# Sliding-window attention with sinks, then an erf-softplus FFN: the first two groups' keys and queries loaded two tokens to a partition

## The chip, the cores and the metric

One core of a Trainium2 chip runs the whole program. The metric is the device time of one execution in microseconds (us); smaller is better. A core has five engines that run side by side and wait for one another by semaphores: PE (TensorE, matmuls; PEld is its weight load), DVE (VectorE), ACT (ScalarE), POOL (GpSimd) and SP (SyncE, which here only issues transfers). Each engine takes its instructions in the order in which the program lists them.

## The reference

Batch 4, 8 heads, 768 tokens, 64 elements per head; 4 sink tokens and a window of 128. All arrays are fp32 in the reference; the two weights reach the kernel as 8-byte numbers.

```python
scores = q @ k^T / sqrt(64)
keep   = (key position < n_sink) | (0 <= query - key < window)
a      = softmax over the kept keys
x      = (a @ v), heads side by side: 3072 tokens x 512
h      = x @ w_in                      # 512 -> 2048
g      = h * erf(softplus(h))
out    = g @ w_out                     # 2048 -> 512
```

## The kernel before

The tokens are worked in 12 groups of 256 (`GT`); a batch element has three groups. A group's attention runs in four steps, one for each pair of heads, so step s belongs to group s // 4; there are 48. A step consists of `prep` (transposes of keys and queries on PE, copied by ACT into `kq`), `core` or `score` (scores on PE; on DVE a predicated copy, then one instruction per block that adds the mask and takes the minimum; the exponential on ACT), `norm` (division by the sum), `ptrans` (weights transposed on PE, copied by ACT into `pa` and `pz`, triangles cut by POOL), `av` (product with the values) and `xfin` (copy into `xf`, later `xh` and `xl`). In group 0 and the other groups that begin a batch element the first 16 keys are also copied behind each block of keys (`SW`), since every query sees the sinks.

Beside it the FFN of a group runs in 16 slices of the hidden width: `hidden` (PE), `act` (ACT for tanh and squares, DVE for the polynomial) and `project` (PE). For the first two groups it works in plain fp32 with one copy of each weight (`wf`); for the others with two rounded parts (`wt`). The 32 weight blocks are loaded as 512 KB of 8-byte numbers (`wload`) and put together to fp32 by three integer instructions each on DVE (`wconv`, L543 to L551).

The order of each engine's work comes from a planner that simulates a timeline; the program gives it priorities (`at(a, what)`, with stage a and offset `O`), and `follow(prev, ins)` fixes that an instruction comes behind another on its engine. `mark["t", s]` is the last score instruction of step s on DVE, `mark["s", s]` the last one of its `norm`.

Groups 0 and 1 have early loads of their own. `early_tile` makes one tile for k, q or v of all 8 heads of a group with 128 tokens to a partition block: partition p holds tokens p and 128 + p, in the order (n h d). `early_load` issues two transfers for each, one per block of 128 tokens, in runs of 64 fp32 (256 bytes). The list `head` sets the order in which SP issues them: k and q of heads 0 and 1 (q's first on ACT's queue), of heads 2 and 3, the first weight, k and q of heads 4 to 7, v, eight transfers for the sinks' rows of v (`early_sinks`), four weights, group 1's k and q, and so on. ACT's queue also loads the two scalars n_sink and window, from which DVE makes the masks `mask0`, `mask1` and `mask`; the third mask and the flags are made by `set_rest`.

Of the kernel before, what the change touches and what calls it, by code (L numbers as in the profile page):

```python
# [14 lines left out]
ALU = mybir.AluOpType  # L15
# [4 lines left out]
P = 128  # L20
SW = 16
# [18 lines left out]
NE, AL = 4, 2  # L40
# [12 lines left out]
def kernel(  # L53
# [11 lines left out]
    nc = tc.nc  # L65
    B, H, S, D = q.shape
    NT, DM = out.shape
    DF = w_in.shape[1]
    NPAIR = H // 2
    NC = DM // P  # L70
    NF = DF // P
    GT = 256
    GPB = S // GT
    NG = B * GPB
    NU = 4
    NSTEP = NG * NPAIR
# [54 lines left out]
    def fast_path():  # L131
        with ExitStack() as st:
# [27 lines left out]
            def set_mask(mk):  # L160

                x = nc.vector.tensor_copy(mk[:, P:], kw[:, 256 : 256 + SW])
                if mk is mask:
                    follow(mark["t", 0], x)
                nc.vector.tensor_scalar(mk, mk, -1.0, NEG, op0=ALU.add, op1=ALU.mult)

            def set_rest():

                follow(mark["t", 0], nc.vector.tensor_tensor(mask[:, :P], kw[:, :128], kw[:, 128:256], op=ALU.max))
                set_mask(mask)  # L170
                set_flags(lambda ins: follow(mark["t", 0], ins))

            set_mask(mask0)
            set_mask(mask1)
# [48 lines left out]
            def early_tile(g, nm):  # L223

                t = wpool.tile([P, 2 * DM], F32, tag="wo", name=f"{nm}_early{g}")
                t = early[g, nm] = t.rearrange("p (n h d) -> p n h d", n=2, h=H)
                for c in range(NPAIR):
                    d, cs = stp.setdefault(g * NPAIR + c, {}), slice(2 * c, 2 * c + 2)
                    if nm == "v":
                        d[nm] = [early[0, nm][:, 1, cs] if g else None] + [t[:, n, cs] for n in range(2)]  # L230
                    else:
                        d[nm] = t[:, :, cs]
                return t

            def early_load(g, nm, hs, eng=None):

                t = early[g, nm] if (g, nm) in early else early_tile(g, nm)
                src = dict(q=q, k=k, v=v)[nm]
                for n in range(2):
                    r0 = g * GT + n * P  # L240
                    (nc.sync if n else eng or nc.sync).dma_start(t[:, n, hs], src[0, hs, r0 : r0 + P].rearrange("h p d -> p h d"))

            def early_sinks(z, i, h):

# [42 lines left out]
            def prep(s):  # L287

                g, c = divmod(s, NPAIR)
                d = stp[s]  # L290
                tp = ps_t.tile([P, 4, P], F32, tag="t", name=f"tqk_{s}")
                for j, t in enumerate((d["k"], d["q"])):
                    for i in range(2):
                        nc.tensor.transpose(  # L294
                            out=tp[:, 2 * j + i, :], in_=t[:, i].rearrange("p h d -> p (h d)"), identity=ident
                        )
                nc.scalar.copy(kq[:, c, 1:, :P], tp)  # L297
                if g % GPB == 0:
                    x = tp[:, 0, :SW].rearrange("p (o t) -> p o t", o=1)
                    nc.scalar.copy(kq[:, c, :3, P:], x.broadcast_to([P, 3, SW]))  # L300

            def core(s):

                prev = None
                late = s - AL >= 2 * NPAIR
                if late:
                    prev = av(s - AL)
                if s < NSTEP:
                    score(s, prev)

            def score(s, prev):

# [58 lines left out]
            def norm(s):  # L371
                d = stp[s]
                sm = d["sum"]
                follow(mark["t", 2] if s == 1 else None, nc.vector.tensor_scalar_add(sm, sm, 1.0e-9))
                nc.vector.reciprocal(sm, sm)
                for i in range(2):
                    for h in range(2):
                        p = pst[:, s % RING, i, h, :P]
                        if NM <= s < NA:
                            nc.scalar.mul(p, p, sm[:, i, h : h + 1])  # L380
                        else:
                            nc.vector.tensor_scalar_mul(p, p, sm[:, i, h : h + 1])
                snk = d["snk"] = small.tile([P, 2 * 4 * SW], F32, tag="snk", bufs=2, name=f"snk_{s}")
                x = pst[:, s % RING, :, :, P:].rearrange("p i h t -> p (i h) t").rearrange("p (o n) t -> p o n t", o=1)
                r = sm.rearrange("p i h -> p (i h)").rearrange("p (o n t) -> p o n t", o=1, t=1)
                mark["s", s] = nc.vector.tensor_tensor(
                    snk.rearrange("p (o n t) -> p o n t", o=2, t=SW), x.broadcast_to([P, 2, 4, SW]),
                    r.broadcast_to([P, 2, 4, SW]), op=ALU.mult,
                )
# [89 lines left out]
            def pos(s):  # L479

                return s if s < NE else 3 * s - 6 if s < 2 * NPAIR else 4 * s - 11

            plan = {}
            for s in range(NSTEP + AL):
                if s < NSTEP:
                    for what, fn, a in (
                        ("prep", prep, max(4, s - 1) if NE <= s < 2 * NPAIR else pos(s) - 3), ("norm", norm, pos(s) + 1 + (s == 1)), ("ptrans", ptrans, pos(s) + 2),
                        ("load", load, pos(s) - 4),
                    ):
                        if what == "load":  # L490
                            if s < 2 * NPAIR:
                                continue
                            plan.setdefault(a, []).append(("load", load_v, s))
                        plan.setdefault(max(a, 0 if what == "prep" else -1), []).append((what, fn, s))
                    if s >= 2 * NPAIR:
                        plan.setdefault(pos(s) - 2, []).append(("dup", dup, s))
                    if s // NPAIR % GPB < GPB - 1:
                        plan.setdefault(pos(s) + (2 if s < NE else 1), []).append(("kcopy", kcopy, s))
# [34 lines left out]
            def wconv(n, wn):  # L533
# [9 lines left out]
                first = nc.vector.tensor_scalar(  # L543
                    ti, w[:, :, 1], 0x07FFFFFF, 3, op0=ALU.bitwise_and, op1=ALU.logical_shift_left
                )
                follow(mark["s", 2] if wn < 1 else mark["t", 3] if wn < 3 else mark["s", 3], first)
                follow(mark.get(("c", wn - 2)), first)
                nc.vector.scalar_tensor_tensor(
                    out=ti, in0=w[:, :, 1], scalar=-0x40000000, in1=ti, op0=ALU.bitwise_and, op1=ALU.bitwise_or
# [23 lines left out]
            head = [(early_load, 0, "k", two[0]), (early_load, 0, "q", two[0], nc.scalar)]  # L573
            head += [(early_load, 0, nm, two[1]) for nm in "kq"] + [(wload, order[0])]
            head += [(early_load, 0, nm, four) for nm in "kq"] + [(early_load, 0, "v", slice(0, H))]
            head += [(early_sinks, z, i, h) for z in range(2) for i in range(2) for h in range(2)]
            head += [(wload, n) for n in order[1:4]]
            head += [(wload, order[4])] + [(early_load, 1, nm, slice(0, H)) for nm in "kq"]
            head += [(wload, n) for n in order[5:8]] + [(early_load, 1, "v", slice(0, H))] + [(wload, n) for n in order[8:W0]]
            for x, (fn, *args) in enumerate(head):  # L580
# [2 lines left out]
            for z in range(2):  # L583
                plan.setdefault(0, []).append(("kcopy", lambda s: early_dup(s), z))
            plan.setdefault(2 * NE, []).append(("dup", lambda s: next_dup(), NE))
            plan.setdefault(2, []).append(("prep", lambda s: set_rest(), NSTEP))
            for m in range(-LEAD, NG * NF + LAG + 2):
                a = m + LEAD
                live = 0 <= m < NG * NF
# [255 lines left out]
```

## Time and profile before

| | |
|---|---|
| median of 3 runs | 738.38 us (738.17 to 738.97) |
| the profiled execution | 738.16 us, span 736.5 us |
| busy, share of the span | PE 97%, PEld 81%, ACT 75%, DVE 66%, POOL 29% |
| granted PE clock, mean | 0.997 |

The span is the time from the first to the last instruction that the profiler recorded; the rest of the execution's time lies around it. Busy shares are means over the whole span and hide that the engines' loads differ by stage. In a line of the timeline the first two numbers are the start and the duration in us; "x4" is the number of instructions merged, and the bracket at the end is the idle time of the engine ahead of them and what ended it. Instructions of PE overlap, so the duration of several in a row is less than the sum of single ones.

### The profile page before, as it was taken

Reading aid. Unit: us, or ns where it says so; the run is one execution under the profiler, and the core shown is the slowest. Engines: PE = TensorE matmul, PEld = TensorE weight load, DVE = VectorE, ACT = ScalarE, POOL = GpSimd, SP = SyncE. Lnnn points to the kernel's source line nnn. Section 1 sums busy time; section 2 is a strip of 40 time slices with the busy share of each in tenths; the row PEclk is TensorE's granted clock in tenths of the full one; section 3 lists DMA queues with packets and bytes.
Section 4 is the critical chain, followed back from the end, with each engine's and each line's share of the span. In section 5 each row is a group of like instructions: output and inputs, shape, how many; then the busy total and the mean of one; then the engine's idle time right before and its main releaser. Section 6 shows DMA issues by size and latency. Waiting matters only on the chain. (4 is left out here: it accounts for less than half of the span.)

```text
span 736.5 us, 16405 instructions
## 1 busy us (share of the span) xinstructions
PE 716.0 (97%) x5808; PEld 595.6 (81%) x5808; DVE 485.3 (66%) x1367; ACT 551.9 (75%) x1313; POOL 210.1 (29%) x302
## 2 busy tenths in 40 slices
PE   6889999999999999999999999999999999999997
PEld 3666567767888888888888888888898888898885
DVE  7999997665776765665666666665566566475252
ACT  4687759976986876976976975985886886777573
POOL 3411332111323322332333232233224223233221
PEclk9999999999999999999999999999999999999999
DMA  7999011121222122212212211311321221200000
GB/s 175 279 347 377 22 37 55 31 57 40 72 48 69 45 54 48 65 43 57 67 41 56 75 38 44 84 36 40 78 48 37 79 58 35 67 13 2 29 1 34
DMA packets 113001, 53.07 MB, mean 72 GB/s; under 512 B 91728, under 2 KB 105552, under 8 KB 112912
## 3 DMA queue, kind: packets, MB, share of 16 engines
q1 hardware_dynamic: 112352, 51.87, 26.3%
q8 instruction: 49, 0.80, 0.5%
q14 instruction: 40, 0.33, 0.1%
q10 hardware_dynamic: 560, 0.07, 0.1%
HBM read 38.01 MB, written 6.29 MB: 60 GB/s over the span
## 5 line engine op out<-in xcount | busy, mean ns | idle before, releaser
L645 PE MATMUL h<-xh,wt 128*128 128x256 f32 x1408 | 277.9, 285 | 0.2 <-DVE u L667 0.2
L645 PEld LDWEIGHTS h<-xh,wt 128*128 128x128 f32 x1408 | 224.0, 188 | 7.6 <-issue 1.7
L675 POOL TENSOR_TENSOR g<-u,g 128x512 fp32r<-128x512 f32 x80 | 106.2, 1327 | 339.3 <-DVE g L674 335.4
L645 PE MATMUL h<-xl,wt 128*128 128x256 f32 x704 | 198.2, 282 | 0.0
L663 ACT ACTIVATE u<-r 128x512 f32<-128x512 f32 x288 | 161.5, 622 | 12.7 <-DVE gf L667 4.7
L645 PEld LDWEIGHTS h<-xl,wt 128*128 128x128 f32 x704 | 132.2, 188 | 5.0 <-issue 1.2
L667 DVE SCALAR_TENSOR_TENSOR u<-u,u 128x512 f32<-128x512 f32 x160 | 124.5, 778 | 16.0 <-ACT u L663 1.8
L691 PE MATMUL o<-wt,g 128*128 128x512 f32 x320 | 127.4, 398 | 0.0
L690 PE MATMUL o<-wt,g 128*128 128x512 f32 x320 | 127.3, 398 | 0.0
L692 PE MATMUL o<-wt,g 128*128 128x512 f32 x320 | 123.6, 397 | 0.2 <-POOLq L813 0.2
L667 DVE SCALAR_TENSOR_TENSOR u<-u,h 128x512 f32<-128x512 f32 x80 | 54.9, 686 | 84.5 <-ACT u L663 82.3
L416 POOL TENSOR_SCALAR_AFFINE_SELECT pz<-pa 64x256 f32<-64x256 f32 (+1 forms) x96 | 54.5, 567 | 150.8 <-ACT pa L405 147.5
L367 ACT ACTIVATE pst<-pst,neg 128x144 f32<-128x144 f32 x192 | 77.4, 407 | 24.9 <-DVE neg L363 23.9
L658 ACT ACTIVATE r<-h 128x512 f32<-128x512 f32 x96 | 56.7, 591 | 17.9 <-PE h L645 14.4
L690 PEld LDWEIGHTS o<-wt,g 128*128 128x128 f32 x320 | 60.0, 187 | 11.5 <-ACT ot L696 0.4
L692 PEld LDWEIGHTS o<-wt,g 128*128 128x128 f32 x320 | 59.0, 188 | 12.5 <-POOLq L813 0.7
L691 PEld LDWEIGHTS o<-wt,g 128*128 128x128 f32 x320 | 60.0, 188 | 10.5
L674 DVE CAST g<-u 128x512 fp32r<-128x512 f32 x80 | 34.6, 432 | 46.3 <-PE o L692 43.6
L659 ACT ACTIVATE r<-r 128x512 f32<-128x512 f32 x96 | 60.7, 632 | 2.5
L660 ACT ACTIVATE r<-r 128x512 f32<-128x512 f32 x96 | 60.7, 632 | 2.5
L687 PE MATMUL o<-wf,gf 128*128 128x512 f32 x128 | 58.3, 594 | 1.2 <-DVE gf L667 1.2
L297 ACT COPY kq<-tqk 128x512 f32<-128x512 f32 x48 | 27.9, 582 | 32.6 <-PE tqk L294 30.2
(88 smaller groups left out, 939.2 us busy)
## 6 DMA issues: line engine op xcount, KB each, us to landing
ws<-in_moe_w_in_dram SPq DMA_DIRECT2D x16, 512.0 KB, 6.0
ws<-in_moe_w_out_dram SPq DMA_DIRECT2D x16, 512.0 KB, 8.3
out_dram<-ot SPq DMA_DIRECT2D x24, 256.0 KB, 2.1
v<-in_v_dram SPq DMA_DIRECT2D x56, 96.0 KB, 2.2
q<-in_q_dram SPq DMA_DIRECT2D x80, 64.0 KB, 2.1
k<-in_k_dram SPq DMA_DIRECT2D x80, 64.0 KB, 2.1
vz<-v SPq DMA_DIRECT2D x80, 64.0 KB, 2.1
kq<-kq SPq DMA_DIRECT2D x28, 64.0 KB, 2.0
```

Source lines behind the costliest of these rows:

```text
L367: nc.scalar.activation(y, y, AF.Exp, bias=d["neg"][:, i, h : h + 1], scale=-1.0, accum_out=d["sum"][:, i, h : h + 1])
L645: last = nc.tensor.matmul(o, wt[NC * j + c][:, p, fs], xt[e][:, c, :], start=(m == 0), stop=(m == len(ops) - 1))
L658: nc.scalar.activation(r, h, AF.Tanh, bias=b_t, scale=0.5)
L659: nc.scalar.activation(r, r, AF.Square, bias=b_v, scale=-0.5)
L660: nc.scalar.activation(r, r, AF.Square, bias=b_r)
L663: sq = nc.scalar.activation(u, r, AF.Square, bias=b_a[i], scale=CS)
L667: pr = nc.vector.scalar_tensor_tensor(out=acc, in0=u, scalar=CC[i] * CS**2, in1=x, op0=ALU.add, op1=ALU.mult)
L675: nc.gpsimd.tensor_tensor(gl, acc, gh.bitcast(F32), op=ALU.subtract)
L687: nc.tensor.matmul(o, gt[0][:, ws], wf[16 + f], start=(f == 0), stop=(f == NF - 1))
L690: behind(nc.tensor.matmul(o, gh[:, ws], wt[16 + f][:, 0, :], start=(f == 0), stop=False))
L691: nc.tensor.matmul(o, gh[:, ws], wt[16 + f][:, 1, :], start=False, stop=False)
L692: nc.tensor.matmul(o, gl[:, ws], wt[16 + f][:, 0, :], start=False, stop=(f == NF - 1))
```

## The change

Four things. (1) The early tiles of k and q get the order (h j d): partition p holds tokens 2p and 2p + 1 of the group, side by side, so that one transfer of runs of 512 bytes loads all 256 tokens. v stays as it was. (2) In `prep` of steps 0 to 7 the four transposes of 128 columns of weights become eight matmuls with the identity, each with 64 columns of weights (one head, one of the two tokens of a partition), written to the upper or lower half of the partitions. Even tokens then lie apart from odd ones, and the copies put them in order: one for k and one for q, each with a stride of two elements in `kq`, and the sinks' copy in the same way. (3) The order: step 0's scores come behind step 1's transposes; the third mask and the flags come behind step 2's score instructions and not step 0's, and one stage later; step 0's `norm` comes behind step 1's score instructions and a stage later, while step 1's `norm` loses the same two conditions; the first weight conversion may come behind step 2's score instructions in place of its `norm`. (4) In the list `head` two of the weights move ahead of the sinks' rows.

```diff
@@ set_mask, set_rest
-                    follow(mark["t", 0], x)
+                    follow(mark["t", 2], x)
...
-                follow(mark["t", 0], nc.vector.tensor_tensor(mask[:, :P], kw[:, :128], kw[:, 128:256], op=ALU.max))
+                follow(mark["t", 2], nc.vector.tensor_tensor(mask[:, :P], kw[:, :128], kw[:, 128:256], op=ALU.max))
                 set_mask(mask)
-                set_flags(lambda ins: follow(mark["t", 0], ins))
+                set_flags(lambda ins: follow(mark["t", 2], ins))
@@ early_tile
-                t = early[g, nm] = t.rearrange("p (n h d) -> p n h d", n=2, h=H)
+                if nm == "v":
+                    t = t.rearrange("p (n h d) -> p n h d", n=2, h=H)
+                else:
+                    t = t.rearrange("p (h j d) -> p h j d", h=H, j=2)
+                early[g, nm] = t
...
-                        d[nm] = t[:, :, cs]
+                        d[nm] = t[:, cs]
@@ early_load
+                if nm != "v":
+                    x = src[0, hs, g * GT : (g + 1) * GT].rearrange("h (p j) d -> p h (j d)", j=2)
+                    (eng or nc.sync).dma_start(t[:, hs].rearrange("p h j d -> p h (j d)"), x)
+                    return
                 for n in range(2):
                     r0 = g * GT + n * P
-                    (nc.sync if n else eng or nc.sync).dma_start(t[:, n, hs], src[0, hs, r0 : r0 + P].rearrange("h p d -> p h d"))
+                    nc.sync.dma_start(t[:, n, hs], src[0, hs, r0 : r0 + P].rearrange("h p d -> p h d"))
@@ prep
+                if s < 2 * NPAIR:
+                    prev = None
+                    for n, t in enumerate((d["k"], d["q"])):
+                        for j in range(2):
+                            for h in range(2):
+                                prev = mark['k', s] = follow(prev, nc.tensor.matmul(
+                                    tp[64 * h : 64 * h + 64, 2 * n + j, :], t[:, h, j], ident, start=True, stop=True
+                                ))
+                    for n in range(2):
+                        y = kq[:, c, 1 + 2 * n : 3 + 2 * n, :P].rearrange("p b (t j) -> p b j t", j=2)
+                        nc.scalar.copy(y, tp[:, 2 * n : 2 * n + 2, :].rearrange("p j (b t) -> p b j t", b=2))
+                    if g % GPB == 0:
+                        y = kq[:, c, :3, P:].rearrange("p n (t j) -> p n t j", j=2)
+                        x = tp[:, :2, : SW // 2].rearrange("p (o j) t -> p o t j", o=1)
+                        nc.scalar.copy(y, x.broadcast_to([P, 3, SW // 2, 2]))
+                    return
@@ core
-                    score(s, prev)
+                    score(s, mark['k', 1] if s == 0 else prev)
@@ norm
-                follow(mark["t", 2] if s == 1 else None, nc.vector.tensor_scalar_add(sm, sm, 1.0e-9))
+                follow(mark["t", 1] if s == 0 else None, nc.vector.tensor_scalar_add(sm, sm, 1.0e-9))
@@ the plan
-                        ... ("norm", norm, pos(s) + 1 + (s == 1)), ...
+                        ... ("norm", norm, pos(s) + 1 + (s == 0)), ...
@@ wconv
-                follow(mark["s", 2] if wn < 1 else mark["t", 3] if wn < 3 else mark["s", 3], first)
+                follow(mark["t", 2] if wn < 1 else mark["t", 3] if wn < 3 else mark["s", 3], first)
@@ head
+            head += [(wload, n) for n in order[1:3]]
             head += [(early_sinks, z, i, h) for z in range(2) for i in range(2) for h in range(2)]
-            head += [(wload, n) for n in order[1:4]]
+            head += [(wload, order[3])]
...
-            plan.setdefault(2, []).append(("prep", lambda s: set_rest(), NSTEP))
+            plan.setdefault(3, []).append(("prep", lambda s: set_rest(), NSTEP))
```

## Rows read from the trace of the kernel before

**Rows 1.** Busy time by stage; columns stand in the first line.

```profile
core 0: us, PE busy (x) PEld busy (x) DVE busy (x) ACT busy (x) POOL busy (x), PEclk, DMA share, GB/s
5.00:16.50 11.50, 9.41 (x66) 5.41 (x66) 8.71 (x55) 6.25 (x26) 3.19 (x6) 1.00 0.81 180
16.50:26.00 9.50, 6.50 (x77) 4.20 (x77) 9.21 (x41) 8.25 (x32) 4.15 (x10) 0.97 1.11 312
26.00:49.00 23.00, 20.25 (x154) 15.65 (x153) 21.83 (x50) 16.96 (x44) 7.54 (x13) 0.94 0.97 305
49.00:86.00 37.00, 35.19 (x202) 23.14 (x203) 36.72 (x94) 26.98 (x71) 5.53 (x8) 1.00 0.73 260
...
200.00:731.00 531.00, 530.76 (x4450) 465.37 (x4449) 323.46 (x906) 399.31 (x924) 159.58 (x217) 1.00 0.20 47
```

**Rows 2.** Timeline of DVE between 5 and 17 us.

```profile
5.05 0.17 DVE L95 CAST tiny<-tiny 128x4 f32<-128x4 int32 x1 [1.22 <-DMA tiny<-in_window_dram]
...
8.31 0.63 DVE L358 COPY_PREDICATED ps<-tri,ps 64x128 f32<-64x128 int8 x2
...
9.89 0.29 DVE L169 TENSOR_TENSOR mask<-kw 128x128 bf16<-128x128 f32 x1
...
11.13 0.17 DVE L374 TENSOR_SCALAR sum<-sum 128x4 f32<-128x4 f32 x1 [0.17 <-ACT pst L367]
...
16.53 0.76 DVE L358 COPY_PREDICATED ps<-tri,ps 64x64 f32<-64x64 int8 x4 [2.09 <-PE ps L345]
```

**Rows 3.** Timeline of PE between 6 and 16 us.

```profile
6.45 1.50 PE L345 MATMUL ps<-kq 64*64 64x144 f32 x16 [0.56 <-ACT kq L300]
...
9.49 1.42 PE L294 MATMUL tqk<-ident,k_early 128*128 128x128 f32 x4 [0.70 <-DMA k_early<-in_k_dram]
10.84 1.51 PE L345 MATMUL ps<-kq 64*64 64x144 f32 x16
12.27 1.11 PE L294 MATMUL tqk<-ident,q_early 128*128 128x128 f32 x4
...
13.95 0.48 PE L398 MATMUL tp<-ident,pst 128*128 128x128 f32 x1 [0.56 <-ACT kq L300]
...
14.99 1.51 PE L345 MATMUL ps<-kq 64*64 64x144 f32 x16
```

**Rows 4.** Timeline of the queues of ACT and SP (durations are those of issuing).

```profile
1.76 0.49 ACTq L93 DMA_DIRECT2D tiny<-in_window_dram  x1
...
5.95 1.05 SPq L241 DMA_DIRECT2D q_early<-in_q_dram  x2
...
9.70 4.58 SPq L246 DMA_DIRECT2D vz<-in_v_dram  x8
```

**Rows 5.** Transfers: 10.9 to 11.9 us, 17.2 to 18.8 us, issues to 45 us.

```profile
DMA packets 876, 0.22 MB, mean 220 GB/s; under 512 B 876, under 2 KB 876, under 8 KB 876
...
DMA packets 177, 0.64 MB, mean 399 GB/s; under 512 B 21, under 2 KB 21, under 8 KB 177
...
k_early<-in_k_dram SPq DMA_DIRECT2D x4, 64.0 KB, 2.8
k_early<-in_k_dram SPq DMA_DIRECT2D x2, 128.0 KB, 4.5
```

**Rows 6.** Timeline of PE, two later stretches.

```profile
36.27 0.64 PE L453 MATMUL av<-pz,vz 128*64 128x64 f32 x16
...
44.23 3.72 PE L641 MATMUL h<-xf,wf 128*128 128x256 f32 x16 [0.66 <-DVE gf L667]
```

**Rows 7.** Groups of instructions to 40 us: ACT's copies (busy us, mean ns).

```profile
L297 ACT COPY kq<-tqk 128x512 f32<-128x512 f32 x8 | 4.6, 584 | 6.8 <-PE tqk L294 6.7
...
L466 ACT COPY xf<-av 128x256 f32<-128x256 f32 x4 | 1.5, 374 | 2.2 <-PE av L453 2.2
```

**Rows 8.** Busy time by stage, one microsecond; columns as in rows 1.

```profile
26.00:27.00 1.00, 1.00 (x4) 0.71 (x4) 1.00 (x3) 0.96 (x4) 0.87 (x3) 0.50 0.89 215
```

**Rows 9.** Waits of PE and DVE, 20 to 110 us: total, times, longest.

```profile
PE h L641 <- DVE wf L551: 0.9, 1, 0.9
...
DVE wf L543 <- DMA ws<-in_moe_w_out_dram: 0.5, 1, 0.5
```

More of the change, by code (lines that the diff above doesn't have):

```diff
@@ L486, in fast_path @@
                     for what, fn, a in (
-                        ("prep", prep, max(4, s - 1) if NE <= s < 2 * NPAIR else pos(s) - 3), ("norm", norm, pos(s) + 1 + (s == 1)), ("ptrans", ptrans, pos(s) + 2),
+                        ("prep", prep, max(4, s - 1) if NE <= s < 2 * NPAIR else pos(s) - 3), ("norm", norm, pos(s) + 1 + (s == 0)), ("ptrans", ptrans, pos(s) + 2),
                         ("load", load, pos(s) - 4),
```

## The prediction

> **What bounds the kernel now.** I read the busy time by stage first [rows 1]. From 49 us on PE is busy for 35.19 of 37 us, and from 200 us to the end for 530.76 of 531. So the end is the time at which PE's unbroken work starts, plus that work. Ahead of it another engine is the bound. VectorE (DVE) is busy for 9.21 of 9.5 us between 16.5 and 26, for 21.83 of 23 between 26 and 49, and for 36.72 of 37 between 49 and 86; it converts the 32 weights in those stretches, and PE itself waits for a converted weight, once for 0.9 us [rows 9]. What delays DVE early therefore delays the end, as long as the work handed from DVE to PE and back moves with it. The one stage in which DVE has real room is 5 to 16.5 us: 8.71 of 11.5 us busy.
>
> The second view is DVE's timeline of that stage [rows 2]. It shows when the engine starts and where it stops. DVE starts on the masks at 5.05 us, when the window's word lands, and then has no gap until about 11 us: masks, the first step's score work from 8.31, the third mask and the flags from 9.89. It waits 0.17 us at 11.13 for ScalarE (ACT), and 2.09 us at 16.53 for the scores of step 2. That last wait is the only large one.
>
> The third view, PE's timeline [rows 3], says why. The scores of step 2 start at 14.99. Ahead of them on PE stand the transposes of step 0's weights (13.95, which waited for ACT's copies of the keys), and ahead of these the q transposes of steps 2 and 3 (12.27), the scores of step 1 (10.84), and the k transposes of steps 2 and 3 (9.49, after a wait of 0.70 us for the k transfer). PE goes in order, so a late transfer of keys holds the scores of step 1, and those hold the rest.
>
> The fourth view, the issuing queues [rows 4], says why the transfer is late: each issue takes SP about half a microsecond, and q's last transfers for group 0 go out only from 5.95 us. Later the eight sinks' transfers hold SP for 4.58 us from 9.70, and the next weights wait behind them.
>
> **The change, part by part.**
>
> *Fewer, longer transfers.* Group 0's k and q take six issues instead of twelve (one of them on ACT's queue, before and after). With 1.05 us for two [rows 4], SP reaches the transfers of heads 4 to 7 about 2 us sooner: in place of 5.95 for the last q, around 3.4. The packets go from 256 to 512 bytes. The trace has rates for short packets only (220 GB/s in a stretch of 256-byte ones) and for weights (399 GB/s) [rows 5]; 512 bytes lie between, and I take 290, nearer the short ones, because a fixed time per packet read off these two rates gives that. K and q of the two groups are 2.1 MB: 9.5 us of transfer at 220, 7.2 at 290, 5.3 at 399. So 2 us of transfer time are saved, between 0 and 4. With issue and transfer together the last k and q of group 0 should be there near 7.6 us; the trace shows PE still waiting for the k at 9.49.
>
> *The transposes become eight matmuls with 64 columns of weights.* Before, four transposes take 1.11 us, and one by itself 0.48 [rows 3]: 0.21 apiece. The four become eight of the same 128 moving columns, and they go alternately to the two halves of the array. The nearest row for such halves is the 16 matmuls of 128x64 weights and 64 columns that take 0.64 us [rows 6], 0.03 apiece, while a whole-array fp32 matmul of 256 columns takes 0.22 (16 in 3.72 us), 0.055 per 64 columns. So halves run in pairs, and eight cost what four did: 0. The other bound is that they do not pair: 4 x 0.21 = 0.85 us more per step.
>
> A rule speaks against this part. The Trainium skill, "TensorE: Matmul & The Clock Gate" (Terms), gives fp32 transposes a transpose mode that is four times faster, and "TensorEngine Tiling (Array Packing)" (Restrictions) says that column tiling switches that mode off for fp32; by it the eight would cost four times the old four, 2.5 us more per step. The trace does not bear it out: the plain fp32 matmul costs 0.11 us per 128 columns [rows 6], less than the transposes' 0.21 in the early stage, not more.
>
> *The copies behind them.* One copy of 512 elements (0.58 us) becomes two of 256 (0.37 by the xf copy of that shape) [rows 7], plus the small one as before: 0.16 us more per step, 0.65 for group 0 and as much for group 1. ACT has 5.25 us free of 11.5 in the early stage and 6 of 23 in the one of group 1 [rows 1], so this is covered; without that cover it would be the 0.65. A write with a stride of two elements is not in the trace. Bounds: no cost, or double the copy (0.37 more each, 3 us for group 0), which would still fit in ACT's idle time but would add 0.7 to each step's latency. I take the lower: the copy's rows differ by number of elements. The k copy can also start before q has arrived, a gain that I do not count.
>
> *Step 0's scores behind step 1's transposes.* Before, PE starts step 0's scores at 6.45, behind one transpose of step 1 only [rows 3]. Now step 1's k and q must have landed as well. They are SP's second and third issue, the latter at some 1.9 us. A k transfer of 64 KB lands 2.8 us after its issue, one of 128 KB 4.5 [rows 5], so step 1's q lands between 4.7 and 6.4, the sooner the less stands ahead of it; I take 5. Transposes and copies take some 1.3 us more, the scores start near 6.3 and, with the 1.5 us that they take [rows 3], end near 7.8. DVE does masks until 8.31, so 0.5 us of cover is left: cost 0, and 0.9 by the slower bound.
>
> *The word that starts DVE.* The window's word is issued at 1.76 on ACT's queue, behind q's transfer [rows 4], which now carries twice the bytes: 64 KB more are 0.16 us at 399 GB/s and 0.3 at 220. DVE is gapless behind it, so all of it counts: -0.15, bounds 0 and 0.3.
>
> *The third mask and flags behind step 2's score work, step 0's normalisation behind step 1's.* The 1.07 us from 9.89 were filler while step 1's scores came. Now step 1's score work stands there, and it needs scores 1 at about 9.9. If PE does the transposes of steps 2 and 3 first (k and q landed at 7.6, eight transposes' worth of 1.7 us), the scores of step 1 run from about 8.9 and end near 10.3: -0.3, bounds 0 and 1. Step 0's normalisation no longer waits for ACT: +0.17.
>
> *Two weights ahead of the sinks' rows.* Two issues of half a microsecond move ahead of eight; the sinks are late by 1 us against the old order of these, but all of it lies 2 to 3 us earlier than before. The first weight conversion follows behind step 2's score work, which comes at about 14 us, so all three weights are there. DVE's later wait of 0.5 us for a weight [rows 9] should shrink: +0.3, bounds 0 and 0.5.
>
> *The sum.* The 2.09 us wait goes, because the transposes of step 2 no longer wait for transfers and its scores can be ready near 12.5, when DVE is still at step 1. 2.09 + 0.17 - 0.15 - 0.3 + 0.3 = 2.1 us. The profiled execution took 738.16 us (span 736.5 and 1.7 around it), so 736.1; against the median of 738.38 that is 736.3.
>
> **The rivals.**
>
> *The gain is lost before PE takes over.* The first hidden matmuls need all four steps' outputs, and on that way stand GpSimd's selections and a stretch in which PE runs at the lower level: between 26 and 27 us the granted clock is 0.50, the lower of its two levels (1.2 of 2.4 GHz) [rows 8]. If these hold the first activation where it is, DVE only converts ahead, and what is won is PE's wait of 0.9 us [rows 9]: 737.5. For it: DVE too has a later wait of 0.5 us [rows 9], so it is not the only limit there. Against it: step 1's and 2's softmax, which feed that way, move with DVE.
>
> *More than the wait.* If the stretch at the lower level does not come (PE was busy for only 6.50 of 9.5 us ahead of it, and that need not be so in the new order), what it lacks, (1 - 0.97) x 9.5 + (1 - 0.94) x 23 = 1.7 us of PE time [rows 1], is won besides, on the way to the first activation: 734.6.
>
> *The eight matmuls do not pair.* One mechanism, on PE between 5 and 16.5 us: 3.4 us more for the four steps, while PE has 2.1 us idle there [rows 1]. The wait of DVE stays and grows by 1.3: 739.7. It decides from an extra of about 0.5 us per step on. The rows of halves speak against it.
>
> *The matmuls lose a fourfold mode.* If a plain fp32 matmul takes four times as long per column as the transpose that it replaces, the four steps cost 4 x 2.55 = 10 us more on PE, of which 2.1 fit in its idle time: 746.5. Every row of a plain fp32 matmul speaks against it. This is the rule on the transpose mode above; the trace does not agree with it.
>
> *The long transfers buy nothing.* If 512-byte packets go at the 220 GB/s of the short ones, k and q land no sooner than the issue saves: the last q near 9.5 instead of 7.6. Scores 2 then come around 13.8 and DVE's wait shrinks by 1.2 instead of 2.1: 737.2.
>
> **How the numbers follow.** The forecast of 735.4 to 736.9 has 0.46. More than the wait has 0.12. The two that leave a gain of about 1 us have 0.25 together. Not pairing has 0.15, the lost mode 0.02. A measurement of this kernel can tell about 0.2% from no change, 1.5 us. Faster by more than that: 0.46 + 0.12 = 0.58, and 0.02 of the small gains, 0.60; slower 0.14, which is 0.12 of not pairing (the rest pairs in part) and the lost mode; what is left, 0.26, is the same. The range goes from the larger gain to the non-pairing case: 734.4 to 739.4; the likeliest alone has 735.4 to 736.9.
>
> **What would show it.** Right: DVE's wait of 2.09 us for scores is gone, step 2's score work starts near 14 us instead of 16.5, PE waits for no k transfer near 9.5, the first output matmul at 49 us comes 2 us sooner, the rest is unchanged. Eight early matmuls should take some 1.1 us, the two copies 0.37 each. Wrong: a new wait of DVE for scores 1, eight matmuls above 1.6 us, copies above 0.6, a first word later than 5.4, or a first output matmul still at 49 us.

## The result

The changed kernel takes 749.11 us (median of 4, 748.48 to 749.67) against 738.27 us (median of 4, 737.97 to 738.97): ratio 1.0145, interval 1.0128 to 1.0163. It is 10.8 us slower where 2.1 us faster was forecast, and outside the range.

The windows of the profile after, columns as in [rows 1]:

```profile
5.00:16.50 11.50, 9.48 (x132) 7.25 (x128) 8.66 (x52) 6.08 (x28) 3.14 (x6) 1.00 0.88 249
16.50:26.00 9.50, 4.19 (x32) 2.83 (x32) 9.37 (x46) 7.59 (x29) 5.82 (x5) 0.64 0.97 305
26.00:49.00 23.00, 20.66 (x209) 15.47 (x208) 18.71 (x44) 9.77 (x33) 5.33 (x14) 0.85 0.99 325
49.00:86.00 37.00, 33.14 (x173) 22.96 (x172) 36.72 (x88) 27.98 (x68) 5.00 (x8) 0.91 0.63 224
...
200.00:731.00 531.00, 530.52 (x4496) 465.64 (x4495) 329.55 (x913) 406.99 (x939) 161.07 (x222) 1.00 0.20 49
```

PE has lost 2.3 us between 16.5 and 26 and 2.1 between 49 and 86, and its granted clock is 0.64, 0.85 and 0.91 where it was 0.97, 0.94 and 1.00: it falls to 0.50, the lower of its two levels (1.2 of 2.4 GHz), at 19.2 us, while PE stands from 16.1 to 19.5, and again at 49.9, while it stands from 49.0 to 52.8. DVE, the bound of these stretches, has lost 3.1 us of 23 between 26 and 49. The last stretch is as full as before.

One subtraction of the page's first part sorts the 11.2 us by which the span grew (747.7 against 736.5). PE's busy line before, then after:

```profile
PE 716.0 (97%) x5808; PEld 595.6 (81%) x5808; DVE 485.3 (66%) x1367; ACT 551.9 (75%) x1313; POOL 210.1 (29%) x302
```

```profile
PE 719.5 (96%) x5904; PEld 600.8 (80%) x5904; DVE 486.2 (65%) x1367; ACT 553.0 (74%) x1321; POOL 203.3 (27%) x302
```

Span less busy is PE's idle time: 20.5 us before, 28.2 after. So PE is busy 3.5 us longer and stands 7.7 us longer. Busy time holds both the work and the rate at which it is done; the experiments take the two apart.

DVE's timeline after, the lines that answer to [rows 2] and two later stretches:

```profile
6.51 0.17 DVE L95 CAST tiny<-tiny 128x4 f32<-128x4 int32 x1 [2.68 <-DMA tiny<-in_window_dram]
...
9.90 0.63 DVE L382 COPY_PREDICATED ps<-tri,ps 64x128 f32<-64x128 int8 x2
...
12.42 0.76 DVE L382 COPY_PREDICATED ps<-tri,ps 64x64 f32<-64x64 int8 x4 [0.86 <-PE ps L369]
...
15.76 0.35 DVE L382 COPY_PREDICATED ps<-tri,ps 64x64 f32<-64x64 int8 x2
...
39.52 0.43 DVE L567 TENSOR_SCALAR wf<-ws 128x512 int32<-128x512 int32 x1 [3.50 <-DMA ws<-in_moe_w_out_dram]
...
41.11 0.43 DVE L567 TENSOR_SCALAR wf<-ws 128x512 int32<-128x512 int32 x1 [0.56 <-DMA ws<-in_moe_w_out_dram]
...
42.77 0.42 DVE L382 COPY_PREDICATED ps<-tri,ps 64x256 f32<-64x256 int8 x1
```

The wait of 2.09 us for step 2's scores is gone, as forecast. But DVE's first scores start at 9.90 instead of 8.31, so it reaches step 2's at 15.76 instead of 16.53: 0.8 us won, not 2.1. At 39.5 it then stands 3.50 and 0.56 us for the tenth and eleventh weight, where it stood 0.5 us before [rows 9], and step 4's scores (42.77) stand behind these conversions, in order. SP's queue shows when these weights are issued, behind four transfers of v (durations are those of issuing):

```profile
32.20 3.17 SPq L209 DMA_DIRECT2D v<-in_v_dram  x4
35.41 1.44 SPq L555 DMA_DIRECT2D ws<-in_moe_w_out_dram  x3
```

But they are not later than before. These lines of the kernel before are the same issue, step 4's first predicated copy and the tenth conversion:

```profile
36.34 1.42 SPq L531 DMA_DIRECT2D ws<-in_moe_w_out_dram  x3
...
32.00 0.42 DVE L358 COPY_PREDICATED ps<-tri,ps 64x256 f32<-64x256 int8 x1
...
40.29 0.43 DVE L543 TENSOR_SCALAR wf<-ws 128x512 int32<-128x512 int32 x1 [0.49 <-DMA ws<-in_moe_w_out_dram]
```

Before, the weights go out 0.9 us later, and DVE comes to the tenth conversion with step 4's scores done. After, it comes to it at 36.0, with those scores still behind it.

No line of the diff touches these transfers or these conversions' place against step 4's scores. The planner, which lays every engine's order by its own estimates of time, laid it anew: step 4's first predicated copy stood behind seven conversions before and stands behind eleven now.

PE's timeline after, against [rows 3], and the first output matmul (49.16 before, 59.18 now):

```profile
8.30 1.13 PE L369 MATMUL ps<-kq 64*64 64x144 f32 x16
9.61 1.09 PE L305 MATMUL tqk<-ident,k_early 128*64 128x128 f32 x16 [0.18 <-DMA k_early<-in_k_dram]
10.51 1.10 PE L305 MATMUL tqk<-ident,q_early 128*64 128x128 f32 x16
11.54 0.85 PE L369 MATMUL ps<-kq 64*64 64x144 f32 x16
...
15.24 0.66 PE L422 MATMUL tp<-ident,pst 128*128 128x128 f32 x4
...
19.48 1.12 PE L422 MATMUL tp<-ident,pst 128*128 128x128 f32 x4 [3.38 <-ACT pz L435]
...
30.30 1.12 PE L305 MATMUL tqk<-ident,k_early 128*64 128x128 f32 x8
31.21 1.07 PE L305 MATMUL tqk<-ident,q_early 128*64 128x128 f32 x8
...
33.99 0.66 PE L305 MATMUL tqk<-ident,k_early 128*64 128x128 f32 x8
34.47 0.61 PE L305 MATMUL tqk<-ident,q_early 128*64 128x128 f32 x8
35.01 0.66 PE L422 MATMUL tp<-ident,pst 128*128 128x128 f32 x4
...
59.18 3.70 PE L712 MATMUL o<-wf,gf 128*128 128x512 f32 x8
```

The lines at 33.99 to 35.01 are the price of one step. Its eight matmuls leave 16 records, two apiece, and take 0.48 us to the next line and about 0.45 after it: 0.93. The same work before, in two lines at half the clock and two at the full one:

```profile
26.70 0.63 PE L294 MATMUL tqk<-ident,k_early 128*128 128x128 f32 x2
27.12 0.63 PE L294 MATMUL tqk<-ident,q_early 128*128 128x128 f32 x2
...
33.50 0.38 PE L294 MATMUL tqk<-ident,k_early 128*128 128x128 f32 x2
33.72 0.38 PE L294 MATMUL tqk<-ident,q_early 128*128 128x128 f32 x2
```

At the full clock four transposes leave four records and take 0.44, from start to start. Eight matmuls cost 2.1 times as much, 0.49 us more per step; over eight steps 3.9 us. That PE's 3.5 us of extra busy time are these 3.9 does not follow: the stretches at half the clock differ too.

### The profile page after: what moved, and what is told of

Its sections match the earlier page's. It is cut to its first block, busy times and chain, and to the rows that moved or that the text cites. A ratio compares the mean times of both kernels' runs of the same rounds, so it can differ in the third digit from the quotient of the medians.

```text
span 747.7 us, 16610 instructions
## 1 busy us (share of the span) xinstructions
PE 719.5 (96%) x5904; PEld 600.8 (80%) x5904; DVE 486.2 (65%) x1367; ACT 553.0 (74%) x1321; POOL 203.3 (27%) x302
## 5 line engine op out<-in xcount | busy, mean ns | idle before, releaser
L440 POOL TENSOR_SCALAR_AFFINE_SELECT pz<-pa 64x256 f32<-64x256 f32 (+1 forms) x96 | 50.1, 522 | 169.7 <-ACT pa L429 166.4
L387 DVE CUSTOM_DVE_ANT_0 pst<-ps,mask 128x144 f32<-128x144 f32 x192 | 47.8, 304 | 1.4
```

## The experiments

Each kernel is timed beside the kernel before on the same chip (738.3 to 738.6). In brackets stand the ratio to it and its interval. PE's busy and idle time come from each run's page, which is of one execution.

**The two halves of the change, each alone.** One run has the new loads, matmuls and copies with the order conditions and the head of before, the other the reverse.

```
layout:  follow(mark["t", 0], ...) for the masks' rest;  norm 1 behind mark["t", 2];  wf 0 behind mark["s", 2]
         sinks' rows ahead of order[1:4]
order:   early_load and prep as before;  conditions and head as after
```

> The new loads, matmuls and copies, with the old order conditions and the old place of the two weights. If the time is lost by the new order conditions alone (theory order), this runs at or below the kernel before: 736 to 739. If it is lost by the new loads themselves, through the later window word, the tenth weight issued behind four v transfers and what the planner makes of them (theory loads), most of the loss stays: 744 to 750, with a wait of VectorE for the tenth weight of 3 us or more.

> The old loads, transposes and copies, with the new order conditions and two weights ahead of the sinks' rows. Theory order: 746 to 750, with ScalarE's copy of step 0's weights held behind step 2's exponential and a stretch of PE at half clock behind 19 us. Theory loads: 736 to 740, the window's word back at 5.0 us.

layout 749.58 us (1.0154, 1.0137 to 1.0171), order 742.19 (1.0057, 1.0040 to 1.0074). The run order lies between its two ranges. Most of the loss shows where the new operations are, but 11.1 and 3.7 do not add to 10.8, and the planner lays each of these runs anew, so neither is one half alone. In layout DVE waits 2.37 us for a weight at 41.31, with step 4's copy behind it at 41.77: another order with the same fault.

**Taking single waits away from the kernel after.**

```
w0_11:    W0, WQ = 11, 10           # tenth and eleventh weight ahead of the v transfers
pa0first: step 2's first exp follows step 0's pa copy (ACT)
t4first:  conversions from the tenth on follow mark["t", 4] (DVE)
win:      (early_load, 0, "q", two[0])     # first q on SP's queue: the window word earlier
oldnorm_t4: t4first, with step 0's and 1's norms conditioned as before
```

> The changed kernel with the tenth and eleventh weight issued ahead of the v transfers; the order on VectorE, ScalarE and PE is the same. If VectorE's 4 us of waiting for these two weights near 36 to 41 us (with step 4's scores queued behind them) sets the end: 744 to 746. If the end is set by PE's half clock and its late transposes: 748 to 750, with the wait gone and the first output matmul still near 59 us.

> The changed kernel with ScalarE's copies of step 0's transposed weights ahead of step 2's first exponential, where they wait 2.8 us now; nothing else moves. If PE's idle time behind 16 us and the half clock that follows set the end: 743 to 747, and PE's granted clock stays at 1.0 between 19 and 26 us. If VectorE's wait for the tenth weight sets it: 748 to 750.

> The changed kernel with one more order condition: weight conversions from the tenth on come behind step 4's score instructions on VectorE. Theory queue (VectorE's in-order wait for the tenth weight holds step 4's scores, ScalarE's exponentials behind them hold the first tanh): step 4's score instructions near 38 to 40 us and not 47, the first tanh near 44 and not 48.8, the time 743 to 745. Theory clock (PE runs at half clock and is the limit anyway): 748 to 750.

> The changed kernel with the first q transfer on SP's queue and not on ScalarE's, so that the window's word has only the other scalar ahead of it. The orders of VectorE, ScalarE and PE are unchanged. If the word's later landing (6.45 against 5.0 us) is passed on in full: the masks start near 4.7 us, 747 to 748. If it is swallowed by the waits behind it: 749 to 750.

> The changed kernel with the old condition on the two first normalisations (which gives back the old order of ScalarE's copies of step 0's weights) and step 4's score instructions ahead of the tenth conversion. Theory queue and theory early order together: 738 to 742. If the loads' landing times cost by themselves: 744 or more.

w0_11 748.71 (1.0140): the wait moves to the twelfth weight (3.10 us at 43.13), which still stands ahead of step 4's second predicated copy. So the place of the v transfers alone is not the loss. pa0first 749.66 (1.0153): PE's gap of 3.38 us becomes two of 1.12 and 1.31, but a wait of 4.64 us for ACT follows at 21.3, and the granted clock is 0.50 from 21.4 to 35.1, as long as in the changed kernel. It takes neither cause away. win 749.17 (1.0143): the word lands at 5.66, and DVE waits 1.44 us for step 0's scores instead. t4first 744.75 (1.0083, 1.0054 to 1.0112) is the one that holds: 4.4 us against the changed kernel, by letting step 4's scores pass the conversions that wait for weights. Its DVE lines:

```profile
37.50 0.90 DVE L382 COPY_PREDICATED ps<-tri,ps 64x256 f32<-64x256 int8 x2 [0.32 <-PE ps L369]
...
41.75 0.43 DVE L567 TENSOR_SCALAR wf<-ws 128x512 int32<-128x512 int32 x1 [1.71 <-DMA ws<-in_moe_w_out_dram]
```

Its first output matmul still stands at 59.71, so that row does not measure the end. oldnorm_t4, 745.83 (1.0098), gives nothing more and lies above the 738 to 742 of its first theory.

**The compute part with the old loads.** b_mmcp has eight matmuls of 64 columns in place of the transposes, and the copy in two halves; the planner orders.

```
nc.tensor.matmul(tp[64*h : 64*h + 64, 2*j + i, :], t[:, i, h], ident, start=True, stop=True)
nc.scalar.copy(kq[:, c, 1 + 2*n : 3 + 2*n, :P], tp[:, 2*n : 2*n + 2, :])
```

> The kernel before with its own loads and order conditions, but the first eight steps' transposes as eight matmuls of 64 columns of weights and the copy in two halves (in the old layout, contiguous). If the new PE and ScalarE work, or the order that the planner makes of it, is what costs: 742 to 749. If the loads cost: 737 to 740.

742.87 (1.0063, 1.0038 to 1.0087): the compute part alone, with the window word at 5.03 as before, already costs 4.4 us. But here too the planner's order moved.

**Holding the order.** To separate the operations from the planner, a chain of order conditions fixes every instruction of every engine and queue in a given order. A transpose's place goes to its two matmuls, a copy's to its two copies, two loads' to their one, and the reverse.

```
for a, b in zip(held, held[1:]):      # one list for each engine and queue
    follow(a, b)                      # order alone, no wait
```

> The new loads, matmuls and copies, but every engine's and every queue's instructions held in the order that they have in the kernel before (a transpose's place taken by its two matmuls, a copy's by its two copies, two loads' by their one; order conditions and head as before). Theory 1, the planner's order is the loss: the new operations by themselves cost next to nothing, first tanh within 1.5 us of 39.84, first output matmul by 51, 736 to 740 us. Theory 2, the new loads and operations themselves cost it (the late window word, the fuller transfers ahead of the first scores, PE's slower start): first tanh at 46 to 49, 746 to 750 us. In between, 740 to 745, each carries a part.

> The mirror: loads, transposes and copies of the kernel before, order conditions and head of the kernel after, and every engine's and queue's instructions held in the order that they have in the kernel after. Theory 1, the planner's order is the loss: first tanh near 48, first output matmul near 58, 746 to 750 us. Theory 2, the new operations are: 738 to 742 us, first output matmul by 51.

| | order of before | order of after |
|---|---|---|
| operations of before | 738.6 | 752.65 (1.0188, 1.0171 to 1.0205) |
| operations of after | 742.98 (1.0061, 1.0044 to 1.0077) | 749.11 |

Each against its own run of before, the order alone costs 14.1 us with the old operations and 10.8 - 4.4 = 6.4 with the new. The new operations cost 4.4 us in the old order, between the two theories, and are worth 14.1 - 10.8 = 3.3 in the new one, which was laid for them. In old_neworder DVE waits 5.09 us for a weight at 43.90, and step 4's copy comes at 46.85. In new_oldorder PE's idle time is 19.9 us, less than before (20.5), and its busy time is 719.8. So in the profiled execution, which at 741.39 us was the shortest of the four, all that is lost is busy time, 3.8 us more.

Busy time is not work, however: old_neworder, with the old transposes, is busy for 719.3 us, 3.3 more than before and as long as the changed kernel. An estimate of the work at one rate takes off half of the busy time at the lower rate, since rows at the two rates differ by 1.8 to 2.0 times (scores 1.51 and 0.85, four transposes 0.85 and 0.44). It counts as lower the busy time in the stretches with a granted clock of 0.50, and that in the early stretch up to the trace's first record of the clock, whose durations are of that rate too (last section):

| | PE busy, us | of it at the lower rate | less half of that |
|---|---|---|---|
| before | 716.0 | 15.7 | 708.2 |
| new_oldorder | 719.8 | 16.8 | 711.4 |
| old_neworder | 719.3 | 25.9 | 706.4 |
| after | 719.5 | 18.6 | 710.2 |

By it the new operations add 3.2 us of work in the old order and 3.8 in the new, near the 3.9 worked out from the rows. The estimate is good to some 2 us: before and old_neworder do the same work and differ by 1.8. In the order of after more of the busy time is at the lower rate, with the old operations (25.9 us) above all.

**What stretches DVE in the held order.** Four lines of new_oldorder on DVE, then two of POOL:

```profile
9.79 0.63 DVE L399 COPY_PREDICATED ps<-tri,ps 64x128 f32<-64x128 int8 x2
...
11.57 1.02 DVE L164 CAST mask<-kw 128x16 bf16<-128x16 f32 x1
...
12.68 1.01 DVE L167 TENSOR_SCALAR mask<-mask 128x144 bf16<-128x144 bf16 x1
...
15.66 0.76 DVE L399 COPY_PREDICATED ps<-tri,ps 64x64 f32<-64x64 int8 x4
```

```profile
11.41 1.14 POOL L265 COPY vz<-v_early 64x1024 f32<-64x1024 f32 x1 [0.29 <-DMA v_early<-in_v_dram]
12.61 1.03 POOL L267 COPY vz<-v_early 64x1024 f32<-64x1024 f32 x1
```

The cast and the subtraction of the masks' rest took 0.17 and 0.18 us before. Here each ends with one of POOL's copies of v.

```
hand:  DVE: the masks' rest and flags behind step 2's scores;  ACT: step 3's kq copy and step 0's pa ahead of step 1's exps
hand_word: hand, with the window word ahead of q on ACT's queue
compute_oldorder: b_mmcp in the order of before
hand2: hand, with two of the masks' instructions behind step 0's scores, the others behind step 3's
nodup: new_oldorder without POOL's two copies of v (early_dup); vz zeroed whole
hand3: DVE: step 1's scores behind step 0's, then norm 0; the masks' rest behind step 3's.  PE: scores 2, 3 ahead of step 0's transposes
```

> As the run with the new operations in the order of before, with three moves made by hand: on DVE the rest of the masks and the flags behind step 2's scores (step 0's norm and step 1's scores no longer stand behind them), on ACT step 3's keys-and-queries copy and step 0's pa copy ahead of step 1's exps. Theory 1 (what is lost under a held order is an order that does not fit the new arrival times): PE's gap at 16.6 goes, the granted clock stays above 0.9 up to 26, first output matmul by 50.5, 737 to 740 us. Theory 2 (the new loads start the scores 1.5 us late and nothing gives that back): first output matmul at 51 to 53.5, 740 to 743 us.

> As the run before it in this call, with the window word's load ahead of the first query load on ACT's queue. If the late word sets DVE's first predicated copy, that copy starts 0.5 to 1.3 us earlier than there and the time falls by as much; if the first scores set it, since their query load is now the later one, nothing changes by more than 0.5 us or it is slower.

> The loads of before, the first eight steps' transposes as eight matmuls and their copies in two halves, every engine's and queue's order held as before. If the loads carry the 4.4 us that the new operations cost in that order: 737.8 to 739.5 us, first scores' predicated copy at 8.3. If the matmuls and copies carry it: 741 to 744 us with that copy still at 8.3, and PE or ACT late behind it.

> As the run with the three moves by hand, but the rest of the masks split: its first two instructions behind step 0's scores (where DVE waited 1.25 us), the others and the flags behind step 3's. If PE's gap of 3.48 us at 17 to 20.5 and the half clock behind it carry what is left: the gap under 2 us, first output matmul by 51, 737.5 to 739.5 us. If the late word and scores carry it whatever the order: 740.5 to 742 us.

> The new operations in the order of before, without POOL's two copies of the first group's v (so its attention is not the reference's in the rows that these copies fill with v). If DVE's long instructions are a collision with these copies: the masks' cast and subtraction take 0.2 us each in place of 1.0, step 1's predicated copy starts near 14 in place of 15.66, 740 to 741.5 us against 743. If they are long for another reason: unchanged, 742 to 744.

> The new operations; on DVE step 1's scores directly behind step 0's (they read PSUM, and ran unharmed beside POOL's copies before), then step 0's norm, step 2's scores, and most of the masks' rest behind step 3's; on PE the scores of steps 2 and 3 ahead of step 0's transposes; on ACT step 3's copy ahead of step 1's exps. If the collision with POOL and the masks' rest carry what hand2 still lost: step 2's scores end by 18.0 (before 18.5), first output matmul by 50, 737.5 to 739 us. If PE's half clock carries it whatever DVE's order: 739.5 to 741.5.

hand is 741.00 (1.0029, 1.0019 to 1.0039), with its first output matmul at 52.61, both as its second theory said. nodup is 740.79 (1.0038, 1.0024 to 1.0052): 2.5 us above before instead of 4.4, in intervals that just overlap. Its DVE lines show the collision gone, as the first theory said:

```profile
11.55 0.17 DVE L164 CAST mask<-kw 128x16 bf16<-128x16 f32 x1
...
11.82 0.17 DVE L167 TENSOR_SCALAR mask<-mask 128x144 bf16<-128x144 bf16 x1
...
14.09 0.76 DVE L399 COPY_PREDICATED ps<-tri,ps 64x64 f32<-64x64 int8 x4
```

compute_oldorder is 741.59 (1.0037, 1.0025 to 1.0050), so by the medians the matmuls and copies carry 3.1 of the 4.4 us and the loads 1.3; the intervals of the two runs overlap, so the 1.3 is not clear of the scatter. Its first scores start on time, at 8.28; PE is 4.7 us busier (720.7, in the longest execution of the six) and idle as before (20.4). Two DVE lines show how a little lateness is enlarged:

```profile
12.10 0.17 DVE L402 TENSOR_SCALAR sum<-sum 128x4 f32<-128x4 f32 x1 [1.17 <-ACT pst L395]
...
12.52 2.42 DVE L410 TENSOR_SCALAR pst<-pst,sum 128x128 f32<-128x128 f32 x4
15.16 0.76 DVE L386 COPY_PREDICATED ps<-tri,ps 64x64 f32<-64x64 int8 x4
```

The norm starts 0.97 us later than before (11.13 [rows 2]). It thereby falls under POOL's copies, and its four products take 2.42 us where they took 0.87; step 1's scores come at 15.16 in place of 12.65. That is 0.97 + 1.55 = 2.5 us.

hand2 gives 740.18 (1.0019, 1.0009 to 1.0028): the best of all with the new operations, between its two theories (PE's gap shrank to 2.40 us only), and still slower than before. PE's idle time is 19.5 us in hand2, a microsecond less than before, and its busy time 719.0, three more. hand_word, 742.74 (1.0048), is worse: the word, issued first, still lands at 6.38, and the scores come a microsecond later, as its second theory allowed. hand3, 742.32 (1.0053), missed both expectations. DVE no longer waits for scores (step 2's start at 16.10), but POOL's selections now meet DVE's conversions, and PE waits 3.47 us for them:

```profile
22.06 0.68 POOL L457 TENSOR_SCALAR_AFFINE_SELECT pz<-pa 64x128 f32<-64x128 f32 x2 [3.70 <-ACT pa L446]
22.81 4.65 POOL L457 TENSOR_SCALAR_AFFINE_SELECT pa<-pa 64x128 f32<-64x128 f32 x2
```

**The half clock, not settled.** Two runs fill PE's gap (16.1 to 19.5 us after, 17.1 to 19.5 in hand2) with matmuls that nothing reads, orders held.

```
for _ in range(30):                   # 20 in hand2_warm
    nc.tensor.matmul(ts4[:, 1, :], ident, ident, start=True, stop=True)
```

> The kernel after, every engine's and queue's order held, with 30 matmuls of the identity that nothing reads behind step 0's last transpose (PE's gap at 16.1 to 19.5). If the half clock carries part of the 10.8 us: granted clock 0.9 or more up to 26 us, the last copy of xf near 38 in place of 40.6, 745 to 748 us. If DVE's order carries it all: the clock rises, the last copy of xf comes earlier, and the time stays at 748.5 to 749.5, because DVE still reaches step 4's scores behind the tenth and eleventh weight.

> As hand2, with 20 such matmuls behind step 3's scores (PE's gap at 17.1 to 19.5). If the half clock carries what hand2 still lost: granted clock 0.9 or more up to 26 us, first output matmul by 50, 736.5 to 738.8 us, no slower than the kernel before. If not: the clock rises and the time stays at 739.5 to 741.

after_warm 750.37 (1.0156), hand2_warm 744.35 (1.0083), both slower than either of their theories. The clock between 16.5 and 26 us rose to 1.00 in both, but the filler was twice too long, because a matmul is two records here as well:

```profile
15.94 6.86 PE L443 MATMUL ts<-ident 128*128 128x128 f32 x60
```

30 matmuls took 6.86 us, 0.229 apiece, and held ACT's copies of the same tile for 2.96 us (3.83 in hand2_warm). So what the half clock between 19 and 33 us costs stays open.

## Why the prediction was wrong

**The step that failed first: "halves run in pairs, and eight cost what four did: 0".** I counted records as matmuls and compared across two rates. A plain fp32 matmul leaves two records, a transpose one. The row of 16 [rows 6] is eight matmuls, 0.08 us apiece and not 0.03, and the hidden row is eight of 0.465, so 128 columns cost 0.23 us and not 0.11. The transposes' 0.21 to 0.28 [rows 3] were those of the slow rate; at the fast one they cost 0.11. The halves do run together (eight half-wide matmuls in 0.93 us, four whole ones at 0.229 in 0.92), but a plain fp32 matmul takes 2.1 times a transpose. The term 0 measures 0.49 us per step at full clock, and 0.95 at half: before, two transposes from 26.70 take 0.42 at a granted clock of 0.50, four 0.85; after, four matmuls from 30.30 take 0.91, eight 1.8. At full clock that is 3.9 us for eight steps, on the engine that sets the end; between kernels of one order the estimate above finds 3.2 and 3.8.

The rule that I set aside spoke for this. The Trainium skill, "TensorE: Matmul & The Clock Gate" (Terms), gives fp32 a faster transpose mode, and "TensorEngine Tiling (Array Packing)" (Restrictions) says column tiling switches it off. The trace agrees on the direction; the factor here is 2.1, where the page has four. The rival that priced non-pairing (0.85 us per step at the slow rate, 739.7) charged four steps of the eight; it had nearly the right size by another mechanism. The rival of the lost mode had the right mechanism at four times the price in four steps; that its 746.5 lies near the measured time is luck, since more than half of the measured loss is the order's.

**The step that failed most: "as long as the work handed from DVE to PE and back moves with it".** The sum ended at DVE's early waits and took the order behind them as given. The planner laid every engine anew. In the changed kernel 7.7 of the 11.2 us are idle time of PE, and the order alone costs 6.4 us by the table. In t4first 4.4 us come back when step 4's scores no longer stand behind conversions that wait for their weights. What the rest is made of, and how much of it is the lower rate, was not taken apart.

**"-0.15" for the word, "cost 0" for step 0's scores, "-0.3" for scores 1.** The word lands 1.46 us later (6.51), and in t4first, with the same loads, as late as 7.25. Its place behind q is at most a part of this: issued ahead of q it took 5.0 us to land instead of 3.2 (hand_word), and with q on the other queue 4.3 (win). Step 0's scores start at 8.30 instead of 6.45, not at 6.3. The k of heads 4 to 7 lets PE go on at 9.61, not at 7.6: it is issued 2.1 us sooner, as forecast, but its one transfer of 256 KB took 6.6 us to land where one of 128 KB had taken 4.5. DVE then waits 0.86 us for scores 1. The term's own figures (7.6, 1.7 us of transposes, 1.5 of scores) end at 10.8 and not at 10.3, which is 0.9 late. In the held order the loads cost 1.3 us by the medians, not clear of the scatter.

**The wait of 2.09 us** went. What came of it in the kernel was 0.8 us at step 2's scores. In hand2, with a fitting order, PE's idle time is 1.0 us less than before: this is the gain, against 3 us of work.

**The copies** were right: 0.34 us each (0.68 for two). Of the signs of being wrong, "a first word later than 5.4" came first, then the new wait for scores 1. Of the rivals none had an order laid anew.

## What to carry to other kernels

Before a row prices an operation, count its records against the code (how many instructions does the loop issue?) and compare rows of one rate only. If PE's last stretch is unbroken, sort a change in span into PE's busy time, at each of its rates, and its idle time first; an operation that grows on that engine adds its length unless waits of the same engine go with it (in hand2 1.0 us of them, against 3 us). Where a planner orders by its own times, hold the old order and run the new operations in it, and the reverse: a change is judged by both runs, and a conversion that waits for a transfer belongs behind the scores, not ahead of them (here 4.4 us).

## What the hardware showed

Two engines stretch each other: DVE's cast and subtraction on bf16 took 1.02 and 1.01 us instead of 0.17 and 0.18 beside POOL's copies, its scaling of fp32 2.42 instead of 0.87; the other way round, POOL's two selections took 4.65 us in hand3 beside DVE's conversions, and 0.68 at 17.69. Predicated copies and score instructions, which read PSUM, kept their length over the same copies before (12.65 to 14.4 us). The Trainium skill, "SBUF — State Buffer" (Who interferes with whom), says that VectorE in one of its two-port modes contends with GpSimd for a pair of ports, which the one that issues first holds for its whole instruction while the other stands. The trace agrees in that cast and subtraction each end with one of POOL's copies, and take 0.17 us each in nodup, without the copies. Which mode they run in no run shows.

The column of the granted clock reads 1.00 from 5 to 16.5 us in both kernels, yet the durations there are of two rates: before, scores take 1.51 us and four transposes 1.11 as late as 16.84, and at 19.09 four transposes take 0.82; after, the scores at 11.54 take 0.85 and the transposes at 15.24 0.66. The trace's records of the clock begin at 18.65 us before and at 8.93 after, and the column reads 1.00 where it has none; at these two times the durations change. So the early stage ran at the slower rate, before for twice as long as after, although the column does not say so.

The window's word, 1 KB, took 4.3 to 5.4 us from issue to landing in the fifteen runs whose first loads carry 128 KB each in rows of 512 bytes, and 3.2 in the five whose loads carry 64 KB in rows of 256.
